# Attention pooling with divided GpSimd additions, pairwise additions instead of reductions on VectorE, and expert weights loaded from a later step

## The chip, the cores and the metric

The kernel runs on one core of a Trainium2 chip. The metric is device time in microseconds (us) of that core, from several executions; one further execution was profiled. The engines are TensorE (PE in the profile, its weight loads PEld), VectorE (DVE), ScalarE (ACT), GpSimd (POOL) and SyncE (SP), which here only issues DMA transfers. SBUF is the on-chip memory, PSUM the memory into which TensorE writes.

## The reference, cut to what matters

Attention over pooled keys and values is followed by a mixture of experts in which every token goes to one expert.

```python
# q, k, v: 8 batches, 8 heads, 576 tokens, 64 dims
k_p = k.reshape(B, H, 72, 8, D).mean(axis=3)      # 8 neighbours pooled
v_p = v.reshape(B, H, 72, 8, D).mean(axis=3)
attn = softmax(q @ k_p.T / sqrt(D))               # 576 x 72 for each head
x = (attn @ v_p) -> tokens x 512                  # 4608 tokens
logits = x @ w_gate; e_idx = argmax(logits, axis=1)
for e in range(8):
    out[e_idx == e] = gate * eom * (relu(x[e_idx == e] @ w1[e]) @ w2[e])
```

## The kernel before

The program has two parts. The first, written in one long order by hand (`attention_and_routing`, up to about 194 us of the profile), computes attention for 36 tiles of 128 tokens and finds each token's expert. The second (`experts`) runs the expert matmuls, for about 460 us.

The first part walks half-steps: tile i, half a of the heads (a is 0 or 1). In one half-step TensorE makes the scores of a tile, transposes the probabilities of the tile two steps back, and multiplies those of three steps back with the pooled values. VectorE takes the row maximum `m` (L242), the reciprocal `grec` (L280) and the normalised output `xg` (L286); ScalarE takes the exponentials. What is not part of every half-step is put between: `plan` holds functions by step (`at(step, f, ...)`), and `queue` holds generators of VectorE work (`pooled`, `route`) from which `work(n)` takes the next n pieces at three places of a half-step. A batch has 4.5 steps; batch b begins at step f.

Pooling of a batch b from 1 on is done as follows.

- Keys lie as 128 partitions x 4 head pairs x 8 positions x 72 columns (`k_t[b]`, named kq in the trace). `pool_k` on GpSimd (L181, L182, step f - 5.5) adds the upper half of the positions to the lower, three times, in place.
- Values lie as 128 partitions x 2 halves of the heads x 3 chunks x 512 columns (`vt`, named rows in the trace; 512 is 8 positions x 64 dims). `halve_v` on GpSimd (L196, step f - 2.5) adds positions 4 to 7 to 0 to 3, one addition for each half of the heads. `pooled` then reduces the four remaining positions on VectorE, one `tensor_reduce` for each chunk and half (`pool_v`, L199), six pieces of `queue` from step f - 2.
- `vt` is one buffer for all batches, so the loads of the next batch's values (`load_v`, L166) wait on SyncE for the last of these reductions, and the loads of q and k behind them in SyncE's order wait too.

Batch 0 is pooled by VectorE alone (`ready_k`, `first_v`), since nothing else can run before. The routing of a group of four tiles (`route`) is a chain of small VectorE operations: among them `d` (L307) and `cand` (L311), both with two inputs in SBUF, and the scalar addition to `gden` (L336). When it has found the places, GpSimd scatters the group's rows to memory (L395, an indirect DMA each).

`stage_in` (L410) loads 512 KB pieces of the first expert's weights into six stage buffers; their split into two parts by ScalarE and VectorE begins at step 26.

Of the kernel before, what the change touches and what calls it, by code (L numbers as in the profile page):

```python
# [15 lines left out]
ALU = mybir.AluOpType  # L16
AX = mybir.AxisListType
PSUM = bass.MemoryType.PSUM

B, H, S, D = 8, 8, 576, 64  # L20
# [57 lines left out]
def attention_and_routing(ctx, tc, sh, qT, kT, v, wg, wst, xs):  # L78
    nc = tc.nc
# [12 lines left out]
    vt = sh.rows[:, 0:6 * DM].rearrange("p (a c f) -> p a c f", a=2, c=3)  # L92
# [61 lines left out]
    k_t, vp_t, vT_t = {}, {}, {}  # L154
# [20 lines left out]
        nc.sync.dma_start(k_t[0][:, 2:4], k[:, 2:4])  # L175
        nc.sync.dma_start(q_t[0][:, :, P:S], q[:, :, P:S])

    def pool_k(b, eng, c0=0, c1=4):
        k = k_t[b][:, c0:c1]
        for w in (4, 2):  # L180
            eng.tensor_tensor(k[:, :, 0:w], k[:, :, 0:w], k[:, :, w:2 * w], op=ALU.add)  # L181
        eng.tensor_tensor(k[:, :, 0], k[:, :, 0], k[:, :, 1], op=ALU.add)  # L182

    def scale_k(b, c0=0, c1=4):
        for h in range(2):
# [3 lines left out]
    def ready_k(a):  # L189
        pool_k(0, nc.vector, 2 * a, 2 * a + 2)  # L190
        scale_k(0, 2 * a, 2 * a + 2)

    def halve_v(b):
        vp_t[b] = p2.tile([P, 3, 2, D], F32, tag="vp", name=f"vp{b}", bufs=1)
        for a in range(2):
            nc.gpsimd.tensor_tensor(vt[:, a, :, 0:256], vt[:, a, :, 0:256], vt[:, a, :, 256:512], op=ALU.add)  # L196

    def pool_v(b, a, c, n=1, w=4):
        nc.vector.tensor_reduce(vp_t[b][:, c:c + n, a], vt[:, a, c:c + n, 0:w * D].rearrange("p c (r d) -> p c d r", r=w),  # L199
                                axis=AX.X, op=ALU.add)  # L200

    def first_v(a):
        if a == 0:
            vp_t[0] = p2.tile([P, 3, 2, D], F32, tag="vp", name="vp0", bufs=1)
        pool_v(0, a, 0, 3, 8)

    def place_v(b, c):
        for h in range(2):
# [261 lines left out]
    def at(step, f, *args):  # L470
        plan.setdefault(step, []).append((f, args))

    def pooled(b):
        for a in range(2):
            for c in range(3):
                pool_v(b, a, c)
                yield 0

    tick = [0]
# [15 lines left out]
    for b in range(1, B):  # L495
        f = S * b // P + 0.5 * (b % 2)
        at(f - 8.5, load_k, b)
        at(max(f - 5, 0), load_v, b)
        at(f - 4.5, load_q, b)
        at(f - 5.5, pool_k, b, nc.gpsimd)  # L500
        at(max(f - 2.5, 1.5), scale_k, b)
        at(f - 2.5, halve_v, b)
        at(f - 2, lambda b: queue.insert(0, [pooled(b), 0, -1]), b)
        for c in range(3):
            at(f - 0.5 + 0.5 * c, place_v, b, c)
        at(f - 0.5, turn_v, b)
        at(f + 1.5, gate_v, b)
    for c in range(STAGES):
        at(3 + 0.5 * c, stage_in, c)
    for c in range(8):  # L510
        at(26 + 1.5 * c, split_hi, c)
        at(27 + 1.5 * c, split_lo, c)
# [13 lines left out]
    prepare_counts()  # L526
    ready_k(0)
    first_v(0)
    at(-0.5, ready_k, 1)
    at(-0.5, first_v, 1)  # L530
    at(1.5, prepare_routing)
    for c in range(3):
# [603 lines left out]
def program():  # L1136
# [12 lines left out]
    with ExitStack() as st:  # L1149
# [27 lines left out]
        with tile.TileContext(nc) as tc:  # L1177
            with ExitStack() as ctx, tc.manual_schedule():
                attention_and_routing(ctx, tc, sh, qT, kT, v, wg, wst, xs)
# [24 lines left out]
```

## Time and profile before

| | |
|---|---|
| Time, 3 runs | median 656.69 us, 655.51 to 657.07 |
| Profiled execution | 657.38 us; its span, first to last instruction, 655.7 us |
| Mean granted TensorE clock | 0.987 |
| Busy over the whole span | PE 93%, PEld 84%, DVE 54%, ACT 40%, POOL 34% |

The span is what the views of the profile show; about 1.7 us lie around it. A share of busy time is a mean over two quite different parts: VectorE is busy 54% of the whole, but nearly without a gap in the first part, where the change lies.

### The profile page before, as it was taken

How to read it: one execution, taken by the hardware profiler on the slowest of the kernel's cores; microseconds unless marked ns; L12 is line 12 of the kernel's file. 1: busy time of each engine (PE TensorE's matmuls, PEld its weight loads, DVE VectorE, ACT ScalarE, POOL GpSimd, SP SyncE). 2: the span in 40 equal slices, each digit the busy share in tenths (PEclk: the TensorE clock that was granted, in tenths of full speed). 3: DMA queues.
4: the chain of work that ended last, by engine and by line, in shares of the span. 5: the costliest groups of instructions: out<-in, count | busy, mean ns of one | idle time of the engine just before them, and what ended most of it. 6: DMA issues, size and time to landing. Idle time of an engine off the chain costs nothing.

```text
span 655.7 us, 11906 instructions
## 1 busy us (share of the span) xinstructions
PE 606.7 (93%) x3715; PEld 553.3 (84%) x3716; DVE 357.3 (54%) x805; ACT 260.0 (40%) x693; POOL 220.6 (34%) x270
## 2 busy tenths in 40 slices
PE   0798898989978999999989999999999899999996
PEld 0697897888877999799788989989898798989895
DVE  5789999899883822578545513265133632222221
ACT  1776886888441511347244402244031421211110
POOL 3557558662532421231404222141213213030213
PEclk9999999999998999999989999999999899999999
DMA  9898687783545931467836422064204112020203
GB/s 258 278 305 289 205 292 276 254 251 114 169 159 191 321 109 44 149 214 254 286 127 233 133 92 73 32 212 141 96 1 158 33 44 93 16 76 32 77 32 90
DMA packets 28746, 101.72 MB, mean 155 GB/s; under 512 B 4735, under 2 KB 5759, under 8 KB 26882
## 3 DMA queue, kind: packets, MB, share of 16 engines
q1 hardware_dynamic: 18194, 61.93, 29.4%
q0 software_dynamic: 10480, 39.03, 17.5%
q14 instruction: 51, 0.42, 0.2%
q8 instruction: 21, 0.34, 0.2%
HBM read 79.67 MB, written 22.58 MB: 156 GB/s over the span
## 4 chain that ended last, share of the span: by engine, by line
PE 64%; issue 2%; DVE 1%; DMA 1%; ACT 0%; DVEq 0%; POOL 0%; ACTq 0%; POOLq 0%
PE p_y L854 31%; PE p_h L873 31%; PE p_x L835 2%; DMA stage<-wst 1%; DVE w1a L998 1%; PE p_y L835 0%; DVE w1b L998 0%; DVE rows L1004 0%; ACT w2b L945 0%; POOL out L1115 0%; ACT w1b L945 0%; ACT xt L938 0%; DVE ht L1011 0%; DVEq L803 0%; PE p_y L915 0%
## 5 line engine op out<-in xcount | busy, mean ns | idle before, releaser
L953 ACT ACTIVATE ht<-p_h 128x384 fp32r<-128x384 f32 (+1 forms) x104 | 46.9, 451 | 264.2 <-PE p_h L873 263.7
L873 PE MATMUL p_h<-xt,w1b 128*128 128x384 f32 (+1 forms) x736 | 117.0, 320 | 5.3 <-issue 5.3
L873 PEld LDWEIGHTS p_h<-xt,w1b 128*128 128x128 f32 x736 | 115.9, 192 | 6.6 <-issue 6.2
L1011 DVE SCALAR_TENSOR_TENSOR ht<-p_h,ht 128x384 fp32r<-128x384 f32 (+1 forms) x104 | 52.5, 505 | 112.9 <-ACT ht L953 112.8
L854 PE MATMUL p_y<-w2a,ht 128*128 128x512 f32 x456 | 108.2, 397 | 5.9 <-issue 4.0
L854 PE MATMUL p_y<-w2b,ht 128*128 128x512 f32 x480 | 111.1, 391 | 0.0
L854 PEld LDWEIGHTS p_y<-w2a,ht 128*128 128x128 f32 x456 | 86.6, 192 | 24.4 <-issue 6.5
L854 PEld LDWEIGHTS p_y<-w2b,ht 128*128 128x128 f32 x480 | 89.5, 188 | 18.4
L873 PE MATMUL p_h<-xt,w1a 128*128 128x256 f32 (+1 forms) x640 | 95.4, 310 | 2.5 <-DVE sums L1024 2.4
L873 PEld LDWEIGHTS p_h<-xt,w1a 128*128 128x128 f32 x640 | 94.3, 193 | 3.5 <-DVE sums L1024 2.6
L1004 DVE TENSOR_SCALAR rows<-p_y,sc 128x512 f32<-128x512 f32 x41 | 30.5, 750 | 120.5 <-PE p_y L854 120.1
L1115 POOL DMA_INDIRECT out<-rows,dst x41 | 41.6, 1015 | 126.1 <-DVE rows L1004 121.4
L247 ACT ACTIVATE p<-p_h,m 128x72 f32<-128x72 f32 x288 | 71.2, 364 | 25.6 <-DVE m L242 25.5
L264 PE MATMUL av<-vbd,pT 128*128 128x162 f32 (+1 forms) x480 | 74.5, 308 | 7.3 <-DVE xg L286 2.4
L264 PEld LDWEIGHTS av<-vbd,pT 128*128 128x128 f32 (+1 forms) x480 | 61.6, 181 | 11.2 <-issue 5.8
L1090 POOL DMA_INDIRECT rows<-xs,src x51 | 59.7, 1171 | 24.2 <-POOL src L1086 13.9
L286 DVE TENSOR_TENSOR xg<-av,grec 128x320 f32<-128x320 f32 x72 | 53.5, 743 | 1.2
L1085 POOL COPY nx<-rows 128x6 f32<-128x6 f32 x17 | 4.2, 245 | 144.7 <-PE p_y L835 71.2
L395 POOL DMA_INDIRECT xs<-xg,where x36 | 36.4, 1012 | 44.0 <-DVE where L350 19.3
L236 PE MATMUL p_h<-kbd,q_even 128*128 128x144 f32 (+1 forms) x160 | 29.3, 310 | 16.1 <-DMA q_even<-qT 12.6
L257 ACT ACTIVATE pT<-ptr 128x384 f32<-128x384 f32 x72 | 38.1, 529 | 4.2 <-PE ptr L256 4.0
L236 PEld LDWEIGHTS p_h<-kbd,q_even 128*128 128x128 f32 (+1 forms) x160 | 23.4, 195 | 17.5 <-issue 12.9
(171 smaller groups left out, 696.4 us busy)
## 6 DMA issues: line engine op xcount, KB each, us to landing
stage<-wst SPq DMA_DIRECT2D x64, 512.0 KB, 5.4
kq<-kT SPq DMA_DIRECT2D x7, 1152.0 KB
rows<-v SPq DMA_DIRECT2D x16, 288.0 KB
kq<-qT SPq DMA_DIRECT2D x4, 1152.0 KB
q_even<-qT SPq DMA_DIRECT2D x3, 1152.0 KB
rows<-v SPq DMA_DIRECT2D x8, 256.0 KB
rows<-v SPq DMA_DIRECT2D x8, 160.0 KB
kq<-kT SPq DMA_DIRECT2D x2, 576.0 KB
```

What stands on the lines that cost most here:

```text
L236: nc.tensor.matmul(s[r0:r0 + n, 144 * c:144 * c + 144], q_t[b][:, 2 * a + c, s0:s0 + n], kbd[b % 2][:, 2 * a + c, :], start=True, stop=True)
L247: nc.scalar.activation(pt[i % 3][:, 4 * a + h, 0:KEYS], sv[:, h], AF.Exp, bias=m[:, h:h + 1])
L257: nc.scalar.activation(pT_t[i][:, 3 * a:3 * a + 3, :], tr[:, 0:384].rearrange("p (c n) -> p c n", c=3), AF.Copy)
L264: nc.tensor.matmul(av[r0:r0 + n, COLS * c:COLS * c + 2 * COLS], pT[:, 3 * a + c, r0:r0 + n], vbd[b % 2][:, a, c].rearrange("p h f -> p (h ...
L286: nc.vector.tensor_tensor(xg[g][:, j, HALF * a:HALF * a + HALF].rearrange("p (f h) -> p h f", h=4), avv[:, :, 0:D + 16], grec[g][:, j, hs] ...
L395: ins = nc.gpsimd.indirect_dma_start(out=xs, out_offset=bass.IndirectOffsetOnAxis(ap=where, axis=0), in_=x.bitcast(I32), in_offset=None)
L854: i = mm(p_y[k], ht[:, h, f, P * k:P * k + P], w[:, part, o:o + DM], start=(f == 0 and part == 0 and h == 0), stop=(f == 7 and h == 1))
L873: i = mm(to, w[:, part, o:o + P], x, start=(d == 0 and k == 0), stop=(d == 3 and k == len(terms) - 1))
L953: act(ht[:, 0, f, 0:size * P], p_h[f % 3][:, 0:size * P], AF.Relu).then_inc(q["hh"], 1)
L1011: nc.vector.scalar_tensor_tensor(ht[:, 1, f, 0:n], src, 0.0, ht[:, 0, f, 0:n].bitcast(F32), op0=ALU.max, op1=ALU.subtract).then_inc(q["hl" ...
L1090: nc.gpsimd.indirect_dma_start(out=xb[:, k].bitcast(I32), out_offset=None, in_=xs, in_offset=bass.IndirectOffsetOnAxis(ap=src[:, k:k + 1], ...
L1115: nc.gpsimd.indirect_dma_start(out=out, out_offset=bass.IndirectOffsetOnAxis(ap=dst[:, k:k + 1], axis=0), in_=yb[k], in_offset=None, bound ...
```

## The change

Three things change, and with them the order in which `queue` hands its pieces to VectorE.

1. `pool_k` on GpSimd makes its first two rounds as one addition for each head pair (`apart=1`): four additions of 288 columns and four of 144 where there was one of 1152 and one of 576. The third round stays one addition. `halve_v` makes six additions of 256 columns where there were two of 768.
2. `pool_v` on VectorE no longer reduces over a strided view. It adds the upper half of the columns to the lower: for batches 1 to 7 two additions for each half of the heads (3 x 128 columns, then 3 x 64 columns into `vp`), four pieces of `queue` instead of six; for batch 0 (`first_v`) three additions of 3 x 256, 3 x 128 and 3 x 64 columns instead of one reduction of 1536 columns.
3. The six `stage_in` are called at steps 14, 15.5, ... 21.5 instead of 3, 3.5, ... 5.5.

```diff
-    def pool_k(b, eng, c0=0, c1=4):
-        k = k_t[b][:, c0:c1]
-        for w in (4, 2):
-            eng.tensor_tensor(k[:, :, 0:w], k[:, :, 0:w], k[:, :, w:2 * w], op=ALU.add)
-        eng.tensor_tensor(k[:, :, 0], k[:, :, 0], k[:, :, 1], op=ALU.add)
+    def pool_k(b, eng, c0=0, c1=4, apart=0):
+        for w in (4, 2, 1):
+            n = apart if apart and w > 1 else c1 - c0
+            for c in range(c0, c1, n):
+                k = k_t[b][:, c:c + n]
+                eng.tensor_tensor(k[:, :, 0:w], k[:, :, 0:w], k[:, :, w:2 * w], op=ALU.add)
...
         for a in range(2):
-            nc.gpsimd.tensor_tensor(vt[:, a, :, 0:256], vt[:, a, :, 0:256], vt[:, a, :, 256:512], op=ALU.add)
-
-    def pool_v(b, a, c, n=1, w=4):
-        nc.vector.tensor_reduce(vp_t[b][:, c:c + n, a], vt[:, a, c:c + n, 0:w * D].rearrange("p c (r d) -> p c d r", r=w),
-                                axis=AX.X, op=ALU.add)
+            for c in range(3):
+                nc.gpsimd.tensor_tensor(vt[:, a, c, 0:256], vt[:, a, c, 0:256], vt[:, a, c, 256:512], op=ALU.add)
+
+    def pool_v(b, a, n):
+        to = vt[:, a, :, 0:n] if n > D else vp_t[b][:, :, a]
+        nc.vector.tensor_tensor(to, vt[:, a, :, 0:n], vt[:, a, :, n:2 * n], op=ALU.add)
...
-        pool_v(0, a, 0, 3, 8)
+        for n in (4 * D, 2 * D, D):
+            pool_v(0, a, n)
...
         for a in range(2):
-            for c in range(3):
-                pool_v(b, a, c)
+            for n in (2 * D, D):
+                pool_v(b, a, n)
                 yield 0
...
-        at(f - 5.5, pool_k, b, nc.gpsimd)
+        at(f - 5.5, pool_k, b, nc.gpsimd, 0, 4, 1)
...
     for c in range(STAGES):
-        at(3 + 0.5 * c, stage_in, c)
+        at(14 + 1.5 * c, stage_in, c)
```

On VectorE, around the pooling of batch 7, the order before was this (`m` is the row maximum, `grec` and `xg` normalise the output, `vp` takes the pooled values, `w1a` is a part of the expert's weights, `lg` and `mx` begin a group's routing):

```order
L242 TENSOR_REDUCE m_1_1940<-p_h 128x4
L199 TENSOR_REDUCE vp_1907<-rows 128x64 x2
L280 RECIPROCAL grec_1729<-av_1_1944 128x4
L199 TENSOR_REDUCE vp_1907<-rows 128x64
L286 TENSOR_TENSOR xg_1727<-av_1_1944,grec_1729 128x4x80
L199 TENSOR_REDUCE vp_1907<-rows 128x64
L425 TENSOR_TENSOR w1a<-stage,w1a 128x512
L242 TENSOR_REDUCE m_0_1969<-p_h 128x4
L199 TENSOR_REDUCE vp_1907<-rows 128x64 x2
L280 RECIPROCAL grec_1979<-av_0_1973 128x4
L301 TENSOR_REDUCE lg_1981<-xg_1727 128x64
```

With the change the same place reads:

```order
L245 TENSOR_REDUCE m_1_2002<-p_h 128x4
L202 TENSOR_TENSOR rows<-rows 128x3x128
L202 TENSOR_TENSOR vp_1965<-rows 128x3x64
L283 RECIPROCAL grec_1787<-av_1_2006 128x4
L202 TENSOR_TENSOR rows<-rows 128x3x128
L289 TENSOR_TENSOR xg_1785<-av_1_2006,grec_1787 128x4x80
L202 TENSOR_TENSOR vp_1965<-rows 128x3x64
L428 TENSOR_TENSOR w1a<-stage,w1a 128x512
L245 TENSOR_REDUCE m_0_2031<-p_h 128x4
L304 TENSOR_REDUCE lg_2033<-xg_1785 128x64
L308 TENSOR_REDUCE mx_2035<-lg_2033 128x4
```

The pooling ends one half-step earlier, and each of its instructions now has two inputs in SBUF; the routing behind it moves up.

On GpSimd, around the halving of batch 4's values, with what each instruction waits for (names in capitals are semaphores of DMA queues; Pool is GpSimd's own), the order before was:

```order
L395 DMA xs<-xg_489,where_866 38913x642
L196 TENSOR_TENSOR rows<-rows 128x3x256 [waits DMAHW5_49,DMAHW6_49,DMAHW4_49,DMAHW7_49,DMAHW1_49,DMAHW0_49]
L196 TENSOR_TENSOR rows<-rows 128x3x256
L395 DMA xs<-xg_734,where_1083 38913x642 [waits DVE_49]
L181 TENSOR_TENSOR kq<-kq 128x4x288 [waits DMAHW3_49,Activation_49]
L181 TENSOR_TENSOR kq<-kq 128x4x144 [waits Pool_49]
L182 TENSOR_TENSOR kq<-kq 128x4x72 [waits Pool_49]
```

With the change it is:

```order
L398 DMA xs<-xg_501,where_878 38913x642
L198 TENSOR_TENSOR rows<-rows 128x256 [waits DMAHW7_49,DMAHW6_49]
L198 TENSOR_TENSOR rows<-rows 128x256 [waits DMAHW1_49,DMAHW0_49]
L198 TENSOR_TENSOR rows<-rows 128x256 [waits DMAHW3_49,DMAHW2_49]
L198 TENSOR_TENSOR rows<-rows 128x256 x3
L398 DMA xs<-xg_754,where_1117 38913x642 [waits DVE_49]
L183 TENSOR_TENSOR kq<-kq 128x288 [waits DMAHW5_49,Activation_49]
L183 TENSOR_TENSOR kq<-kq 128x288 x3
L183 TENSOR_TENSOR kq<-kq 128x144 [waits Pool_49] x4
L183 TENSOR_TENSOR kq<-kq 128x4x72 [waits Pool_49]
```

Nothing changes its place on GpSimd here. The additions of one round now follow each other without depending on each other.

On SyncE's queue, behind the load of batch 2's keys, the order before was (stage is a piece of expert weights, rows a piece of v, q_even q, kq keys):

```order
L158 DMA kq<-kT 128x2304
L147 DMA xs<-stage 1x642
L410 DMA stage<-wst 128x1024 x2
L166 DMA rows<-v 72x2x512
L166 DMA rows<-v 32x2x512
...
L166 DMA rows<-v 72x2x512
L410 DMA stage<-wst 128x1024
L162 DMA q_even<-qT 128x2304
L410 DMA stage<-wst 128x1024
L158 DMA kq<-kT 128x2304
L410 DMA stage<-wst 128x1024 x2
```

With the change these stage loads are gone from here; three stand behind the keys of batch 5, as below, and three behind those of batch 6.

```order
L162 DMA q_even<-qT 128x2304
L158 DMA kq<-kT 128x2304
L413 DMA stage<-wst 128x1024 x3
L166 DMA rows<-v 72x2x512
```

Two loads of 512 KB no longer stand ahead of the values of batch 2, and four no longer around its q and the keys of batch 3.

## Rows read from the trace of the kernel before

**Rows 1.** Busy time by stretch, windows view; (x) counts instructions.
```profile
40.00:60.00 20.00, 17.77 (x143) 15.67 (x143) 18.94 (x54) 13.78 (x52) 10.40 (x7) 1.00 0.89 289
60.00:160.00 100.00, 92.75 (x754) 85.01 (x752) 95.82 (x302) 80.11 (x303) 61.12 (x52) 1.00 0.73 243
```

**Rows 2.** Groups by line and form, VectorE, 19 to 166 us: busy, mean ns | idle.
```profile
L199 DVE TENSOR_REDUCE vp<-rows 128x64 f32<-128x256 f32 x42 | 23.6, 591 | 2.0 <-POOL rows L196 1.9
...
L307 DVE TENSOR_TENSOR d<-lg,mx 128x32 f32<-128x32 f32 x8 | 8.6, 1077 | 0.0
...
L336 DVE TENSOR_SCALAR gden<-gden 128x4 f32<-128x4 f32 x7 | 5.0, 713 | 0.0
...
L311 DVE SCALAR_TENSOR_TENSOR cand<-d,rev 128x32 f32<-128x32 f32 x7 | 3.4, 487 | 0.0
...
L319 DVE TENSOR_TENSOR zs<-lg,oh 128x32 f32<-128x32 f32 x7 | 1.3, 190 | 0.0
```

**Rows 3.** The same view of GpSimd, 19 to 166 us.
```profile
L196 POOL TENSOR_TENSOR rows<-rows 128x768 f32<-128x768 f32 x14 | 25.1, 1818 | 10.4 <-DMA rows<-v 6.6 <-DVE m L242 2.9 <-issue 0.8
L181 POOL TENSOR_TENSOR kq<-kq 128x1152 f32<-128x1152 f32 x7 | 18.5, 2641 | 20.2 <-DMA kq<-kT 20.1
L181 POOL TENSOR_TENSOR kq<-kq 128x576 f32<-128x576 f32 x7 | 9.9, 1414 | 0.5
L182 POOL TENSOR_TENSOR kq<-kq 128x288 f32<-128x288 f32 x7 | 5.6, 797 | 0.5
```

**Rows 4.** The same view of VectorE, 0 to 19 us.
```profile
L199 DVE TENSOR_REDUCE vp<-rows 128x192 f32<-128x1536 f32 x2 | 5.5, 2750 | 5.3 <-DMA rows<-v 5.3
...
L181 DVE TENSOR_TENSOR kq<-kq 128x576 f32<-128x576 f32 x2 | 1.5, 745 | 0.0
L181 DVE TENSOR_TENSOR kq<-kq 128x288 f32<-128x288 f32 x2 | 0.9, 457 | 0.1
```

**Rows 5.** Timeline from 69.7 us: start, duration, engine; like rows merged (xN).
```profile
69.74 2.65 POOL L181 TENSOR_TENSOR kq<-kq 128x1152 f32<-128x1152 f32 x1 [3.35 <-DMA kq<-kT]
...
70.40 1.13 DVE L199 TENSOR_REDUCE vp<-rows 128x64 f32<-128x256 f32 x2
```

**Rows 6.** Timeline from 44.4 us.
```profile
44.46 1.81 POOL L196 TENSOR_TENSOR rows<-rows 128x768 f32<-128x768 f32 x1 [6.65 <-DMA rows<-v]
...
44.93 1.39 DVE L307 TENSOR_TENSOR d<-lg,mx 128x32 f32<-128x32 f32 x1
```

**Rows 7.** Timeline from 62.8 us.
```profile
62.82 3.57 POOL L196 TENSOR_TENSOR rows<-rows 128x768 f32<-128x768 f32 x2
...
63.08 3.37 DVE L307 TENSOR_TENSOR d<-lg,mx 128x32 f32<-128x32 f32 x1
...
67.31 0.41 PE L264 MATMUL av<-vbd,pT 128*128 128x162 f32 x1 [1.57 <-DVE vbd L224]
```

**Rows 8.** Timeline from 101.9 us.
```profile
102.02 3.80 DVE L336 TENSOR_SCALAR gden<-gden 128x4 f32<-128x4 f32 x1
...
102.21 3.58 POOL L196 TENSOR_TENSOR rows<-rows 128x768 f32<-128x768 f32 x2
...
106.83 0.38 PE L264 MATMUL av<-vbd,pT 128*128 128x162 f32 x1 [2.10 <-DVE at L345]
```

**Rows 9.** Timeline from 143.3 us.
```profile
143.42 3.61 POOL L196 TENSOR_TENSOR rows<-rows 128x768 f32<-128x768 f32 x2
...
145.29 1.14 DVE L199 TENSOR_REDUCE vp<-rows 128x64 f32<-128x256 f32 x2
```

**Rows 10.** Timeline from 22.2 us.
```profile
19.59 4.13 POOL L181 TENSOR_TENSOR kq<-kq 128x1152 f32<-128x1152 f32 x2 [10.86 <-DMA kq<-kT]
...
22.76 1.04 DVE L148 CAST tri<-stage 128x128 bf16<-128x128 f32 x1
```

**Rows 11.** Waits of GpSimd, 27 to 75 us: total, times, longest.
```profile
POOL kq L181 <- DMA kq<-kT: 9.3, 3, 4.4
POOL rows L196 <- DMA rows<-v: 6.6, 1, 6.6
```

## The prediction

> **What bounds the kernel now.** I looked first at where the change lies in time: all of it is in the first part, up to about 166 us. The windows view of that part [rows 1] says what bounds it. From 40 to 160 us TensorE is busy 17.77 + 92.75 = 110.5 of 120 us and VectorE 18.94 + 95.82 = 114.8. Both are nearly full, so TensorE can win at most its 9.5 us of idle time there: 2.2 between 40 and 60 us, 7.25 later. The waits view puts nearly all of these on VectorE, in small pieces but for two: 1.57 us at 67.31 [rows 7] and 2.10 us at 106.83 [rows 8].
>
> Next I asked why VectorE is full. In the view by line and form [rows 2] the 42 reductions of pooled values take 23.6 us. Beside them stand small operations with absurd means: `d`, 32 columns, takes 1077 ns on average, while `zs`, the same shape with two SBUF inputs, takes 190. The excess over 190 ns is 8 x 0.89 = 7.1 us for `d`, 7 x 0.30 = 2.1 for `cand`, 7 x 0.52 = 3.7 for `gden`: 12.9 us in all that isn't work.
>
> The timelines say what it is. At 44.93 `d` takes 1.39 us and ends at 46.32, just behind the end (46.27) of a GpSimd addition [rows 6]. At 63.08 `d` takes 3.37 and ends at 66.45, behind the second of two GpSimd additions (66.39) [rows 7]; at 102.02 `gden` takes 3.80 and ends at 105.82, again behind the second (105.79) [rows 8]. The cast at 22.76 is the same picture [rows 10]. So such an operation of VectorE is held while GpSimd adds. A strided reduction is not: at 70.40 two of them take 1.13 us in the middle of a GpSimd addition that runs from 69.74 to 72.39 [rows 5].
>
> This cuts into the change from both sides. It takes 42 instructions that are never held and puts 28 in their place that have two SBUF inputs, like `d`. And it divides the GpSimd instructions that hold.
>
> **The change part by part.**
>
> *VectorE's own work.* An addition with two SBUF inputs took 457 ns for 288 columns and 745 for 576 [rows 4]: 1.00 ns a column and 0.169 us fixed. That gives 0.94 us for 768 columns, 0.55 for 384, 0.36 for 192. A batch's six reductions cost 6 x 0.591 = 3.55 us [rows 2]; four additions cost 2 x (0.55 + 0.36) = 1.83. That is 1.72 less for each of seven batches, 12.0 us of VectorE. For batch 0, 2.75 us [rows 4] become 0.94 + 0.55 + 0.36 = 1.85 without gaps; dependent additions add some 0.04 each, so 0.83 less, twice: 1.65 us.
>
> *The start, -1.1 us.* Both of those reductions stand on VectorE ahead of a row maximum for which ScalarE waits, while GpSimd is still idle (its first addition starts at 19.59 [rows 10]), so nothing holds them. But the cast at 22.76 [rows 10] comes next, and it was released when the second GpSimd addition ended. The first GpSimd addition starts when its keys land, no earlier than now; four additions of 288 columns at 0.80 [rows 3] end at 22.8. The cast would get through at 22.8 instead of 23.8. Bounds: -1.65 (not held) to 0 (held to the end of the second round too, 24.7); I take -1.1.
>
> *The values and keys of batches 2 and 3, -1.5 us.* GpSimd waited 6.6 us for values once and 9.3 in three waits for keys between 27 and 75 us [rows 11], behind the stage loads. These waits cost nothing directly, since pooling is scheduled well ahead. But with 1 MB less in front, the additions on batch 3's keys move ahead of the pooling of batch 2, which they now cover in part, and that pooling is 1.72 us shorter. Of the 2.23 us that TensorE idles between 40 and 60 I give back 1.5. Bounds: -2.2 to 0 (the keys come earlier and hold `d` instead).
>
> *Pooling elsewhere, -0.4 us.* In batches 4 and 5 little or no GpSimd addition lies at the pooling, and the 1.72 us less counts where TensorE waits: in the small pieces, 7.25 - 1.57 - 2.10 = 3.6 us. I take 0.4; bounds 0 and -1.5.
>
> *The new additions held, 0.* In batch 7 the pooling began at 145.29, when the first half's addition was done and the second half's ran until 147.03 [rows 9]; the reductions ran through. The new additions would be held by three pieces of 0.73 us (below): 0.7 to 2.2 us, and I take 1.5. Less the 1.72 saved, that is nothing. Batches 1 and 6 are alike. In batch 3 the pooling lies inside the additions on keys [rows 5]: four pieces of 0.80, held up to 3.2 us, 1.6 in the middle, again nothing net. Bounds for the five places together: -6 (not held) to +5.
>
> *The divided additions on GpSimd.* From 797 ns for 288 columns and 1414 for 576 [rows 3], 2.14 ns a column and 0.18 us fixed: 0.49 us for 144 columns, 0.73 for 256. A batch's keys go from 4.85 to 4 x 0.80 + 4 x 0.49 + 0.80 = 5.96 us, its values from 3.64 to 6 x 0.73 = 4.38: 1.85 us more, 13 us in all. GpSimd is busy 61 of 100 us [rows 1], so this alone costs nothing. What it does to the holds depends on one thing: whether VectorE gets in between two GpSimd additions that follow without a gap. Three times it stood there waiting. Once it got in [rows 6], twice not [rows 7, 8]. Taking one in three, an operation that arrives at the beginning of `halve_v` waits 0.5 + 2 x 0.73 = 2.0 us, where 63.08 and 102.02 waited 3.2 and 3.6. TensorE's two waits of 1.57 and 2.10 would shrink by 1.2 and 1.6. Since the halving also moves against the routing (1.85 us longer a batch, scatters between), I count half of it: -1.4. Bounds: -3.7 and +1.4 (held to the end of all six, 0.7 longer each). For keys the first round grows from 2.64 to 3.2: +0.3.
>
> [...]
>
> *Stage loads at steps 14 to 21.5, 0.* They stand behind keys on SyncE's queue, ahead of values that wait there for VectorE anyway. At 0.73 DMA share from 60 to 160 us [rows 1] there is room for 3 MB, and their first reader is at step 26. If they made values late, GpSimd's slack (its 39 idle us of 100) covers it.
>
> *Sum.* -1.1 - 1.5 - 0.4 + 0 - 1.4 + 0.3 = -4.1. The profiled execution took 657.38 us, span 655.7 and 1.7 around it: 653.3. It lies 0.7 above the median of the runs shown, 656.69; against that the forecast is 652.6 us.
>
> **The rivals.**
>
> *First: VectorE gets in after every piece.* A wait is then at most 0.80 us. Waits grow with the square of the piece: 2.64, 1.41, 0.80 and 3.64 (squares 22.8) become four of 0.80, four of 0.49, 0.80 and six of 0.73 (7.4), so 12.9 us of holds fall to 4.2; new ones, 0.4 at five places, add 2. VectorE has 12.9 - 4.2 - 2 + 12.0 = 18.7 us less, TensorE's 9.5 us of waits mostly go (I take 6.6), and the start gives 1.6: 648.5. For it: rows 6; against it: rows 7, 8. [...]
>
> *Second, slower: VectorE never gets in before a gap.* Keys then hold for 3.2 + 1.96 = 5.2 us (the second round's waits are on additions long done), values for 4.4. Squares: 26.6 + 0.6 + 19.2 = 46.4, twice 22.8, so 12.9 us become 26: +13.3. The pooling is held 2.2 us in batches 1 and 7, 1.6 in 6, 1 in 5, 2.6 in 3: 9.6. Less 12.0, VectorE has 10.9 us more. At 63.08 and 102.02 holds of 6.8 us made TensorE wait 3.67, a share of 0.54: +5.9, less 1.1 at the start: 661.5. It decides from about 2 us more VectorE time on. For it: rows 7, 8; against it: rows 6. [...]
>
> *Third: nothing reaches TensorE.* What VectorE saves is eaten by other holds, and only the start gains, in part: 656.0. Speaking for it is that TensorE itself is 92% busy.
>
> **How the numbers follow.** A change of 0.3% (2 us) is about what a measurement of this kernel can tell from none. The likeliest case 0.45, with 650 to 657 as its own range (three quarters of it below 654.7, a quarter between); the first rival 0.20, the second 0.21, the third 0.14. Faster: 0.34 + 0.20 + 0.02 = 0.56; same: 0.11 + 0.10 + 0.03 = 0.24; slower: 0.20. Leaving out a tenth at either end, the range is 648.3 to 661: to the first rival's time below, just short of the second's above.
>
> **What would show it.** At the start the second row maximum some 1.6 us earlier, and the cast released near 22.8. Four `L202` additions a batch at 0.55 and 0.36 us where GpSimd is idle; longer by whole pieces of 0.73 or 0.80 in batches 1, 3, 6, 7. The mean of `d` and `gden` falls below 1077 and 713 (first rival: under 450; second: over 1500). GpSimd's additions at 0.80, 0.49 and 0.73. TensorE idle from 40 to 160 us near 6.5 instead of 9.5. The prediction fails if VectorE's additions are held for 3 us and more in most batches, or if TensorE's idle time stays though the holds shrink.

## The result and the profile after

The changed kernel took 652.43 us in the median of 20 runs (646.45 to 656.90), the kernel before 656.47 us in as many beside it: a ratio of 0.9937, 95% interval 0.9916 to 0.9958. The forecast was 652.6 us, faster; on a second chip the ratio was 0.9911 (0.9877 to 0.9945). The time came out as forecast. Several terms of the sum did not, and the experiments below are about those.

The profiled execution took 649.39 us, span 647.5, so it is one of the quicker ones. The windows view answers to [rows 1] (columns: window, length, then busy time and instructions of PE, PEld, DVE, ACT and POOL, granted clock, DMA share, GB/s):

```profile
40.00:60.00 20.00, 19.33 (x162) 18.13 (x162) 19.25 (x63) 15.70 (x63) 16.09 (x23) 1.00 0.66 225
60.00:160.00 100.00, 92.14 (x756) 85.96 (x755) 87.76 (x287) 80.34 (x303) 68.71 (x92) 0.98 0.80 270
...
80.00:100.00 20.00, 18.44 (x148) 17.47 (x147) 18.62 (x63) 15.66 (x61) 15.60 (x22) 1.00 1.02 339
100.00:120.00 20.00, 17.81 (x153) 16.39 (x151) 14.57 (x48) 15.43 (x57) 13.77 (x21) 1.00 0.97 332
120.00:140.00 20.00, 18.70 (x140) 17.92 (x142) 18.77 (x59) 15.65 (x59) 16.54 (x22) 0.91 0.79 247
```

From 40 to 60 us TensorE gained 1.6 us of busy time. From 60 to 160 VectorE has 8 us less to do, but TensorE is no busier than before; the DMA engines are full from 80 to 120 us (share 1.02 and 0.97), and the clock, 1.00 in both stretches before, is 0.91 for 20 us.

VectorE at the start, the view by line and form from 0 to 19 us, beside [rows 4]:

```profile
L202 DVE TENSOR_TENSOR rows<-rows 128x768 f32<-128x768 f32 x2 | 1.9, 954 | 4.8 <-DMA rows<-v 4.8
...
L202 DVE TENSOR_TENSOR rows<-rows 128x384 f32<-128x384 f32 x2 | 1.1, 558 | 0.1
...
L202 DVE TENSOR_TENSOR vp<-rows 128x192 f32<-128x192 f32 x2 | 0.7, 357 | 0.1
```

The same view from 19 to 166 us, beside [rows 2]:

```profile
L202 DVE TENSOR_TENSOR rows<-rows 128x384 f32<-128x384 f32 x14 | 10.5, 752 | 5.4 <-POOL rows L198 5.4
L202 DVE TENSOR_TENSOR vp<-rows 128x192 f32<-128x192 f32 x14 | 7.1, 508 | 0.2
...
L310 DVE TENSOR_TENSOR d<-lg,mx 128x32 f32<-128x32 f32 x8 | 3.3, 411 | 0.0
...
L322 DVE TENSOR_TENSOR zs<-lg,oh 128x32 f32<-128x32 f32 x8 | 2.6, 322 | 0.0
...
L339 DVE TENSOR_SCALAR gden<-gden 128x4 f32<-128x4 f32 x8 | 1.8, 222 | 0.0
L314 DVE SCALAR_TENSOR_TENSOR cand<-d,rev 128x32 f32<-128x32 f32 x8 | 1.7, 208 | 0.0
...
L148 DVE CAST tri<-stage 128x128 bf16<-128x128 f32 x1 | 0.4, 391 | 0.0
```

The pooling takes 10.5 + 7.1 = 17.6 us where the reductions took 23.6. Unheld, as at the start, it would be 14 x (0.558 + 0.357) = 12.8, so 4.8 us are holds. The operations that stood out before have shrunk (`d` 1077 to 411 ns, `gden` 713 to 222); `zs` has grown from 190 to 322. That is one execution: in another of the same kernel (e9 below) `d` took 1287.

GpSimd in the same stretch, beside [rows 3]:

```profile
L198 POOL TENSOR_TENSOR rows<-rows 128x256 f32<-128x256 f32 x42 | 30.9, 769 | 3.4 <-DMA rows<-v 3.3
...
L183 POOL TENSOR_TENSOR kq<-kq 128x288 f32<-128x288 f32 x35 | 27.9, 821 | 20.5 <-DMA kq<-kT 13.3 <-ACT p L250 6.6
L183 POOL TENSOR_TENSOR kq<-kq 128x144 f32<-128x144 f32 x28 | 13.4, 506 | 0.0
```

Its waits from 27 to 75 us, beside [rows 11] (line, what it waited for: total, times, longest): the 9.3 and 6.6 us behind DMA are now 2.6 and 0.2.

```profile
POOL kq L183 <- ACT p L250: 6.6, 2, 3.9
POOL kq L183 <- DMA kq<-kT: 2.6, 1, 2.6
...
POOL rows L198 <- DMA rows<-v: 0.2, 1, 0.2
```

The row maximum `m`, once a half-step, dates the lead over before. In these two executions it was 2.9 us at step 6, 8.5 at step 11.5 (the hold of [rows 7] is gone) and 11.8 at step 21 (that of [rows 8] is gone). At step 26 it was 10.6, half a step later 6.8, and 5.5 at the end of the tiles. The other 2.6 us between the two spans lie behind the last row maximum; from there to the end the 14 profiled executions of this document vary from 487.3 to 490.4 us. What took the lead back from step 26 on is on TensorE's timeline (start, duration, engine; idle time before, with its releaser, in brackets):

```profile
116.81 0.99 PE L267 MATMUL av<-vbd,pT 128*128 128x162 f32 x6
120.96 1.10 PE L239 MATMUL p_h<-kbd,q_even 128*128 128x144 f32 x4 [3.16 <-DMA q_even<-qT]
```

And the windows of 2 us there:

```profile
118.00:120.00 2.00, 0.00 (x0) 0.00 (x0) 1.68 (x2) 0.00 (x0) 2.00 (x4) 1.00 1.00 420
120.00:122.00 2.00, 1.04 (x5) 1.06 (x6) 1.48 (x5) 0.00 (x0) 1.84 (x2) 0.79 0.42 175
122.00:124.00 2.00, 2.00 (x10) 2.00 (x9) 1.97 (x6) 1.47 (x6) 1.39 (x3) 0.50 0.63 176
124.00:126.00 2.00, 2.00 (x16) 1.96 (x15) 1.97 (x8) 1.41 (x8) 1.97 (x3) 0.85 0.93 281
126.00:128.00 2.00, 2.00 (x18) 2.00 (x17) 1.90 (x9) 2.00 (x9) 2.00 (x4) 1.00 1.02 301
```

TensorE waits 3.16 us for q (an earlier wait for q, 1.49 us at 98.80, had no lower clock behind it), then works at a granted clock of 0.50 until 124.6 us. In busy time that second loss is invisible: a full 2 us hold 10 matmuls from 122 us on, at 0.50, and 18 from 126, at 1.00.

### The profile page after: what moved, and what is told of

It is laid out like the page before. It is cut to its first block, busy times and chain, and to the rows that moved or that the text cites. A ratio compares the mean times of both kernels' runs of the same rounds, so it can differ in the third digit from the quotient of the medians.

```text
span 647.5 us, 11966 instructions
## 1 busy us (share of the span) xinstructions
PE 603.8 (93%) x3715; PEld 553.9 (86%) x3716; DVE 344.5 (53%) x795; ACT 259.6 (40%) x693; POOL 233.5 (36%) x340
## 4 chain that ended last, share of the span: by engine, by line
PE 67%; issue 2%; DVE 1%; DVEq 0%; POOL 0%; ACT 0%; POOLq 0%
PE p_y L857 33%; PE p_h L876 32%; PE p_x L838 2%; DVE w1a L1001 1%; PE p_y L838 0%; POOL out L1118 0%; DVE rows L1007 0%; DVE xt L994 0%; ACT xt L941 0%; PE p_y L918 0%; DVE sums L1027 0%; DVEq L689 0%; DVEq L1026 0%; DVEq L1038 0%; DVEq L806 0%
## 5 line engine op out<-in xcount | busy, mean ns | idle before, releaser
L876 PE MATMUL p_h<-xt,w1b 128*128 128x384 f32 (+1 forms) x736 | 115.5, 317 | 4.8 <-issue 4.8
L876 PEld LDWEIGHTS p_h<-xt,w1b 128*128 128x128 f32 x736 | 114.4, 189 | 6.1 <-issue 5.7
L1093 POOL DMA_INDIRECT rows<-xs,src x51 | 57.8, 1134 | 24.6 <-POOL src L1089 13.2
L183 POOL TENSOR_TENSOR kq<-kq 128x288 f32<-128x288 f32 (+1 forms) x63 | 41.0, 681 | 20.5 <-DMA kq<-kT 13.3
L239 PEld LDWEIGHTS p_h<-kbd,q_even 128*128 128x128 f32 (+1 forms) x160 | 24.2, 202 | 19.7 <-issue 15.9
```

Source lines behind the costliest of these rows:

```text
L239: nc.tensor.matmul(s[r0:r0 + n, 144 * c:144 * c + 144], q_t[b][:, 2 * a + c, s0:s0 + n], kbd[b % 2][:, 2 * a + c, :], start=True, stop=True)
L876: i = mm(to, w[:, part, o:o + P], x, start=(d == 0 and k == 0), stop=(d == 3 and k == len(terms) - 1))
L1093: nc.gpsimd.indirect_dma_start(out=xb[:, k].bitcast(I32), out_offset=None, in_=xs, in_offset=bass.IndirectOffsetOnAxis(ap=src[:, k:k + 1], ...
```

## The experiments

Each kernel was run on one chip with the kernel before beside it; the ratio is to that. Before took 656.5 us in the median on the first chip and 662.2 to 662.7 on the three others (e1 to e4, e5 to e8 and e9 to e12 on one each), so only ratios are compared. Where two ratios are subtracted, the interval of the difference comes from the two half-widths, added as squares. "Pooling" is the busy time of VectorE's pooling, "d" the mean of `d`, both from 19 to 166 us of the one profiled execution.

| Kernel | GpSimd divided | VectorE adds pairs | Stage loads | Ratio (95%) | Pooling, us | d, ns |
|---|---|---|---|---|---|---|
| before | no | no | 3 to 5.5 | 1 | 23.6 | 1077 |
| e2 | no | no | late | 0.9960 (0.9931 to 0.9989) | 23.5 | 694 |
| e3 | yes | no | 3 to 5.5 | 0.9946 (0.9922 to 0.9969) | 23.2 | 940 |
| e4 | no | yes | 3 to 5.5 | 1.0015 (0.9989 to 1.0041) | 24.9 | 868 |
| e7 | no | yes | late | 1.0020 (0.9995 to 1.0045) | 23.9 | 721 |
| e12 | values only | yes | late | 0.9935 (0.9909 to 0.9961) | 23.2 | 577 |
| changed | yes | yes | late | 0.9937 (0.9916 to 0.9958) | 17.6 | 411 |
| e9, changed again | yes | yes | late | 0.9911 (0.9877 to 0.9945) | 16.9 | 1287 |
| e1 | yes | yes | 3 to 5.5 | 0.9897 (0.9861 to 0.9934) | 15.9 | 671 |
| e5 | yes | yes | spread | 0.9904 (0.9875 to 0.9934) | 16.7 | 745 |
| e6 | yes | yes | last | 0.9880 (0.9842 to 0.9917) | 16.0 | 573 |
| e8 | keys chained | yes | late | 0.9854 (0.9817 to 0.9890) | 17.0 | 397 |
| e10 | keys chained | yes | last | 0.9863 (0.9831 to 0.9894) | 16.8 | 370 |
| e11 | keys chained | yes | spread | 0.9858 (0.9819 to 0.9897) | 17.6 | 323 |

**The parts one by one.** The theory: dividing GpSimd's additions is what gains, and late loads cost; the rivals are that one of the others gains.

e1_early_loads, on the changed kernel:

```diff
-        at(14 + 1.5 * c, stage_in, c)
+        at(3 + 0.5 * c, stage_in, c)
```

> The changed kernel with part 3 undone: the six stage loads are at steps 3 to 5.5 again. Theory (part 3 costs): moved to steps 14 to 21.5 the loads fill the DMA engines (share 1.02 from 80 to 100 us and 0.97 from 100 to 120), q of a late batch lands late, TensorE waits 3.2 us for it and then loses its clock (0.91 from 120 to 140 us). Put back, these go: share from 80 to 120 us near 0.8, no wait on qT over 1 us, 647 to 650 us, 2 to 5 below the changed kernel's 652.4. Rival (part 3 helps): without the late loads the keys and values of batches 2 and 3 are late again, as in rows 11, and the 2.4 us that the changed kernel gained around step 5 go: 654 to 656 us. As predicted (stage loads cost nothing, gain 1.5 us early): 654.

The ratio lies in the theory's range (647 to 650 of 656.5), but not for its reason. A wait for q is there again, at another place (TensorE's timeline, then windows):

```profile
64.30 0.31 PE L239 MATMUL p_h<-kbd,kq 128*64 128x144 f32 x1 [2.68 <-DMA kq<-qT]
```

```profile
62.00:64.00 2.00, 0.00 (x0) 0.00 (x0) 1.74 (x3) 1.61 (x7) 2.00 (x4) 1.00 1.02 417
64.00:66.00 2.00, 1.70 (x15) 1.45 (x16) 1.44 (x5) 0.08 (x1) 1.47 (x2) 0.71 0.89 358
66.00:68.00 2.00, 2.00 (x9) 1.66 (x10) 1.74 (x10) 1.12 (x5) 0.00 (x0) 0.50 0.58 205
```

Here too the DMA engines are full ahead of the wait (share 1.02 from 62 to 64 us) and the clock is halved behind it (0.50 from 66 to 68). So with the loads at either of these two places a late q was possible once the first part ran ahead.

e2_late_loads_alone, on before:

```diff
-        at(3 + 0.5 * c, stage_in, c)
+        at(14 + 1.5 * c, stage_in, c)
```

> The kernel before with part 3 alone (stage loads at steps 14 to 21.5). Theory: the early stretch wins some 1.5 to 2.5 us, the stretch from 100 to 140 us loses 3 to 5 by a late q: 657 to 660 us, a little slower than 656.5. Rival (part 3 is where the gain is): 653 or less. The holds stay as in before: mean of d near 1077 ns, gden near 713.

A miss: faster, not slower. From 40 to 60 us TensorE is busy 19.82 us instead of the 17.77 of [rows 1]; no wait of TensorE for q reached 1 us. The holds did not stay either: `d` fell to 694 ns and `gden` to 548, though nothing was divided. So these means move without a division too; each is of seven or eight operations of one execution.

e3_divided_alone, on before, with the changed `pool_k`:

```diff
-            nc.gpsimd.tensor_tensor(vt[:, a, :, 0:256], vt[:, a, :, 0:256], vt[:, a, :, 256:512], op=ALU.add)
+            for c in range(3):
+                nc.gpsimd.tensor_tensor(vt[:, a, c, 0:256], vt[:, a, c, 0:256], vt[:, a, c, 256:512], op=ALU.add)
...
-        at(f - 5.5, pool_k, b, nc.gpsimd)
+        at(f - 5.5, pool_k, b, nc.gpsimd, 0, 4, 1)
```

> The kernel before with part 1 alone: GpSimd's additions divided, VectorE still reduces. Theory (VectorE gets in between two GpSimd additions): the means of d and gden fall below 450 and 350 ns, cand below 300, TensorE's waits of 1.57 and 2.10 us on VectorE go, 650 to 653 us. Rival (VectorE gets in only at a gap or a wait, and the changed kernel escaped because its routing fell elsewhere): d and gden stay at 1000 and 700 ns or more, and the time at 656 to 659.

The time is 0.54% less, at the weak end of the theory's range. `gden` fell to 360 ns and `cand` to 184, but `d` stayed at 940: the theory is right for most operations and wrong for `d`, which at 131.09 us was held 3.56 us, past five boundaries between additions of keys. TensorE then waited 3.4 us, and the waits behind VectorE that were to go left one of 1.5 us behind `vbd`, at 83.03.

e4_pairs_alone, on before, with the changed `pool_v`:

```diff
-        pool_v(0, a, 0, 3, 8)
+        for n in (4 * D, 2 * D, D):
+            pool_v(0, a, n)
...
-            for c in range(3):
-                pool_v(b, a, c)
+            for n in (2 * D, D):
+                pool_v(b, a, n)
```

> The kernel before with part 2 alone: pairwise additions on VectorE beside whole GpSimd additions. Theory (holds last as long as a GpSimd instruction, or two): the additions by VectorE save 12 us when nothing holds them (0.55 and 0.36 us each), but in batches 1, 3, 6 and 7 they are held for 1 to 3 us at a time, so that their mean lies over 0.9 us and about half of the 12 us is lost: 653 to 656 us. Rival (part 2 is the whole gain): means near 0.55 and 0.36, and 648 to 651 us. Rival the other way (never in before a gap): 658 or more.

No gain at all. The view by line and form shows why, and the timeline one case of it:

```profile
L200 DVE TENSOR_TENSOR rows<-rows 128x384 f32<-128x384 f32 x14 | 12.9, 919 | 0.8 <-POOL rows L196 0.7
L200 DVE TENSOR_TENSOR vp<-rows 128x192 f32<-128x192 f32 x14 | 12.0, 858 | 0.2
```

```profile
69.69 4.32 POOL L181 TENSOR_TENSOR kq<-kq 128x1152 f32<-128x1152 f32 x2 [4.22 <-ACT pT L258]
...
70.08 2.67 DVE L200 TENSOR_TENSOR vp<-rows 128x192 f32<-128x192 f32 x1
...
72.77 1.66 DVE L200 TENSOR_TENSOR rows<-rows 128x384 f32<-128x384 f32 x1
...
75.20 1.06 PE L265 MATMUL av<-vbd,pT 128*128 128x162 f32 x6 [2.64 <-DVE xg L287]
```

Additions of 0.36 and 0.55 us take 2.67 and 1.66 inside GpSimd's additions on keys, where two reductions ran through in 1.13 [rows 5]. In all, 24.9 us instead of 23.6: the whole saving went into holds. What TensorE lost is more than these 1.3 us. The windows view from 40 to 160 us, beside [rows 1]:

```profile
40.00:60.00 20.00, 17.73 (x133) 16.10 (x132) 17.96 (x49) 14.71 (x58) 11.07 (x8) 0.91 0.86 294
...
60.00:160.00 100.00, 89.58 (x700) 83.39 (x699) 88.84 (x268) 73.41 (x276) 60.10 (x50) 0.95 0.72 239
```

TensorE idled 12.7 us instead of 9.5, and its granted clock was 0.91 and 0.95 where before had 1.00 (0.85 and 0.94 in e7 below). This was one of e4's slower executions, 666.1 us beside a median of 663.0.

e7_pairs_late_undivided, on the changed kernel, with `pool_k` as before:

```diff
-        at(f - 5.5, pool_k, b, nc.gpsimd, 0, 4, 1)
+        at(f - 5.5, pool_k, b, nc.gpsimd)
...
-            for c in range(3):
-                nc.gpsimd.tensor_tensor(vt[:, a, c, 0:256], vt[:, a, c, 0:256], vt[:, a, c, 256:512], op=ALU.add)
+            nc.gpsimd.tensor_tensor(vt[:, a, :, 0:256], vt[:, a, :, 0:256], vt[:, a, :, 256:512], op=ALU.add)
```

> The changed kernel with part 1 undone: GpSimd's additions whole again, pairwise additions on VectorE and late loads kept. Theory (part 1 is what makes part 2 pay, by short holds): VectorE's pairwise additions take 0.8 to 0.9 us on average as with part 2 alone, d 800 ns or more, and the time is 0.996 to 1.002 of before. Rival (parts 2 and 3 alone give the gain): 0.994 or less.

As the theory had it: 1.002, pooling means 1106 and 600 ns (`d` lower than expected). Parts 2 and 3 without part 1 gain nothing.

**Which division.** e12_values_divided_only, on the changed kernel:

```diff
-        at(f - 5.5, pool_k, b, nc.gpsimd, 0, 4, 1)
+        at(f - 5.5, pool_k, b, nc.gpsimd)
```

> The changed kernel with whole additions on keys again (1152 and 576 columns) and divided ones on values. Theory (holds cost by the length of a piece, wherever it is): VectorE's pairwise additions in batches 3 and 4 stand inside additions of keys of 2.6 us, as with part 2 alone; mean of the 384-column addition 0.85 us or more, d 700 ns or more, and about half of the gap between the changed kernel (0.994) and the undivided one (1.002) is lost: 0.996 to 1.000. Rival (the division of values carries the gain): 0.995 or less. Rival (that of keys does): 1.000 or more.

The rival wins: with divided values alone the time is that of the changed kernel. The pooling does stand in the keys' long additions, as expected (`d`, 577 ns, came out lower),

```profile
L202 DVE TENSOR_TENSOR rows<-rows 128x384 f32<-128x384 f32 x14 | 15.7, 1123 | 0.9 <-POOL rows L198 0.9
L202 DVE TENSOR_TENSOR vp<-rows 128x192 f32<-128x192 f32 x14 | 7.5, 536 | 0.2
```

yet dividing the keys as well gained no time that these runs can tell. e9 shows what can eat it.

**The same kernel again.** e9_changed_again is the changed kernel without an edit.

> The changed kernel itself, unaltered, beside the next three on one chip. Two questions. First, its time against these: 0.991 to 0.997 of before. Second, its first part: the profiled execution of the changed kernel was 11 us ahead of before at 113 us and lost some 5 of them behind a wait of 3.2 us for q. Theory (q can't come earlier than the DMA engines bring it, so this repeats): again a wait for q of over 1 us between 60 and 125 us with half clock behind it. Rival (that execution was an uncommonly quick one, and the wait came of its lead): a lead of 5 to 8 us at 113 us and no wait for q over 1 us.

The ratio, 0.9911, lies at the lower end of the expected range, and of the two accounts of the wait the rival holds: the lead at step 22.5 (113 us before) was 6.1 us against the same trace of before, which is from another chip, and there was no wait for q over 1 us. It had another loss instead (timeline):

```profile
127.41 4.68 DVE L310 TENSOR_TENSOR d<-lg,mx 128x32 f32<-128x32 f32 x1
127.68 5.70 POOL L183 TENSOR_TENSOR kq<-kq 128x288 f32<-128x288 f32 x9
...
132.87 0.88 PE L267 MATMUL av<-vbd,pT 128*128 128x162 f32 x2 [3.98 <-DVE cand L314]
```

```profile
130.00:132.00 2.00, 0.00 (x0) 0.00 (x0) 2.00 (x1) 0.00 (x0) 2.00 (x4) 0.77 1.05 350
132.00:134.00 2.00, 1.13 (x4) 1.16 (x5) 1.97 (x10) 1.88 (x8) 1.40 (x4) 0.50 1.07 302
134.00:136.00 2.00, 2.00 (x10) 1.99 (x9) 1.97 (x7) 2.00 (x10) 0.00 (x0) 0.50 0.93 334
136.00:138.00 2.00, 2.00 (x14) 1.94 (x13) 0.76 (x5) 2.00 (x9) 0.00 (x0) 0.52 0.27 111
```

`d` waits through six boundaries of the divided additions, longer than any single hold of before, and gets in at the seventh. Divided additions that follow without a gap can act like one long one: `d` took 4.68 us here.

**A gap between the additions.** e8_chained_keys, on the changed kernel: the additions on keys go head pair by head pair, so that most need the one before. The edit also divides the third round, into four additions of 72 columns.

```diff
-        for w in (4, 2, 1):
-            n = apart if apart and w > 1 else c1 - c0
-            for c in range(c0, c1, n):
+        n = apart if apart else c1 - c0
+        for c in range(c0, c1, n):
+            for w in (4, 2, 1):
```

> The changed kernel with GpSimd's divided additions of keys in another order: head pair by head pair (288, 144, 72 columns, each needing the one before) instead of round by round. In the traces so far VectorE always got in where GpSimd waited some 0.08 us between two additions, and of the ungapped boundaries inside the keys it missed about a third. Theory (a gap decides): no operation of VectorE is held past a boundary that has a gap of 0.08 us, so that none of 32 columns takes more than 1.7 us and d comes below 400 ns; 0.989 to 0.994 of before, since one hold less of 1 us is little beside the noise. Rival (it is chance, or what stands behind on GpSimd decides): d is still held past two and more boundaries in a batch.

Every hold inside the keys ends at its first boundary (one less than 0.05 us behind an operation's start is not counted here and below). In the timeline three operations of one routing stand in one series of keys and get through in about half a microsecond each; the longest of all operations of 32 columns up to 166 us takes 1.13 us:

```profile
92.68 4.37 POOL L183 TENSOR_TENSOR kq<-kq 128x144 f32<-128x144 f32 x8
...
93.78 0.60 DVE L310 TENSOR_TENSOR d<-lg,mx 128x32 f32<-128x32 f32 x1
...
95.54 0.57 DVE L318 TENSOR_TENSOR oh<-cand,best 128x32 bf16<-128x32 f32 x1
...
96.15 0.53 DVE L322 TENSOR_TENSOR zs<-lg,oh 128x32 f32<-128x32 f32 x1
```

The gain is more than expected: 0.9854. It is the lowest ratio measured; its interval lies below the changed kernel's first one and overlaps that of e9, from which it differs by 0.0057 (0.0007 to 0.0107). Where the gain comes from is argued, not shown. This profile is no better than the changed kernel's first (TensorE idle 9.4 us from 40 to 160, against 8.5; `d` 397 ns, against 411), only better than e9's (12.7 us and 1287 ns), so the long holds that no longer occur are the likely cause. No run divides the third round without the chain.

**Where the loads go.** e5_loads_spread, on the changed kernel:

```diff
-        at(14 + 1.5 * c, stage_in, c)
+        at(5.5 + 4.5 * c, stage_in, c)
```

> The changed kernel with its six stage loads one by one, each behind a batch's keys (steps 5.5, 10, ... 28), instead of three and three behind the keys of batches 5 and 6. Theory (stage loads next to each other make q late: in the changed kernel TensorE waits 3.2 us for q at 117.8 us and then runs at half clock, with the loads early it waits 2.7 us at 61.6 and then the same): no wait of TensorE for q above 0.5 us between 40 and 160 us, no half clock behind one, and a time of 0.985 to 0.990 of before (the changed kernel 0.994). Rival (a faster first part meets another wait in place of this one, as long): 0.992 to 0.996.

e6_loads_last, on the changed kernel:

```diff
-        at(14 + 1.5 * c, stage_in, c)
+        at((19, 23.5, 27.5, 28, 28.5, 29)[c], stage_in, c)
```

> The changed kernel with its stage loads as late as their readers allow: steps 19 and 23.5, and four behind the last q (27.5 to 29), where the changed kernel's DMA share was 0.33. Theory: as with the loads spread, 0.985 to 0.990 of before, DMA share below 0.9 in every stretch of 20 us from 40 to 140 us. Rival (the loads are now too late for their split, which begins at step 26): a wait of ScalarE or VectorE on stage between 130 and 180 us, and 0.992 or more.

From 40 to 160 us neither waits for q (e5 waits 1.05 us for it at 28.65). Their ratios, 0.9904 (just above the range expected) and 0.9880 (in it), are below the changed kernel's, but the intervals overlap, and e1, which does wait for q, lies at 0.9897. Whether the place of the loads matters is not settled on this base. The rival of e6 did not come: no wait on the stage buffers shows from 130 to 180 us. e6's DMA share reached 0.93 from 100 to 120 us, more than expected, and e5's as well.

e10_chained_loads_last joins the `stage_in` line of e6 to the `pool_k` of e8, e11_chained_loads_spread that of e5.

> Keys added head pair by head pair (as e8) and stage loads as late as their readers allow (as e6), in one kernel. If the two gains add up (0.985 and 0.988 where the changed kernel is at 0.994): 0.979 to 0.984 of before. If both remove the same thing, or are noise of a few profiles: 0.985 to 0.990. No operation of 32 columns is held past a boundary with a gap.

> Keys added head pair by head pair and the stage loads one behind each batch's keys (as e5). As for the kernel with the loads last: 0.980 to 0.986 if the gains add up, 0.986 to 0.990 if not; and within 0.4% of the loads-last kernel either way, since both take the loads out of the way of q.

0.9863 and 0.9858 beside 0.9854 with the loads left late: with chained keys the place of the loads makes no difference that these runs can tell. e10 lies where the gains do not add up, e11 at the border of its two ranges. All three chained kernels lie together.

## Why the forecast was right, and which of its terms were not

The sum, -4.1 us, was met: (1 - 0.9937) x 656.5 = 4.1. Its terms were not those that made it.

**Price of the additions: right.** 954, 558 and 357 ns against 0.94, 0.55 and 0.36; GpSimd's pieces 821, 506 and 769 ns against 0.80, 0.49 and 0.73, the excess being time in which VectorE held them (undisturbed they took 0.79 to 0.82, 0.48 to 0.50 and 0.72 to 0.74, those of 288 and 256 columns 1.04 to 1.11 where a 384-column addition had got in).

**The start, -1.1: near.** The second row maximum came 1.66 us earlier, 1.6 were announced, and the cast began at 22.35 and took 0.39, near the 22.8. Single executions spread: in the eleven with the new start it came 0.82 to 2.18 us earlier than in before, 1.5 in the mean, and in e2 and e3, where the start is untouched, 0.72 and 0.07. Half a step later the eleven were 1.0 us ahead in the mean, and e2 and e3 as before.

**Pairwise additions: about as forecast, but only beside divided ones.** Start, batches 2 and 3 and other pooling were to gain 3.0 together, the new holds being paid for. Beside part 1 they did: from e3 (0.9946) to e1 (0.9897), on one chip, part 2 gains 0.49%, 3.2 us (0.4 to 6.1). Alone it gave +0.15%, or 1.0 us more (0.7 less to 2.7 more, x 662). The forecast let five batches be held for what they saved, 5 x 1.72 us, and the others not at all. With divided additions the 28 new instructions take 3.1 (e1) to 4.8 us more than unheld, less than that; with whole ones 24.9 - 12.8 = 12.1 us, which is all of the 12.0 that they save.

**Divided additions, -1.4 + 0.3: the step that failed, as too small.** Alone they gave -0.54%, 3.6 us (2.1 to 5.2), and beside part 2 more: from e4 (1.0015) to e1 (0.9897), on one chip, 1.18%, 7.8 us (4.8 to 10.8). The forecast took "VectorE gets in one time in three" from three cases. The count over the 14 profiled executions, up to 166 us, is below: operations of VectorE that lasted over 1.2 times their shortest of that execution plus 0.08 us, and the first place in them where one GpSimd addition followed another. Other limits shift the counts by a few.

| Boundary between two GpSimd additions | got in | missed |
|---|---|---|
| any, with a gap of about 0.08 us (the second needs the first) | 74 | 0 |
| whole additions on values, no gap | 6 | 5 |
| divided additions on values, no gap | 98 | 1 |
| divided additions on keys, no gap | 44 | 18 |

So the first rival's mechanism (in after every piece) holds for the divided additions on values (98 of 99), and the second's (not before a gap) for a part of those on keys (18 of 62 missed); after a miss at the keys 28 of the next 46 boundaries were missed too. A gap let VectorE in 74 times of 74. Why the keys miss and the values hardly ever do no run here shows.

**Stage loads, 0, and batches 2 and 3, -1.5: right alone, not on top of the rest.** Part 3 alone gave -0.40%, 2.6 us (0.7 to 4.6), with TensorE 2.05 us busier from 40 to 60 us; that is what the term of 1.5 described. "Room for 3 MB" was read from a mean DMA share of 0.73 over 100 us, while the six loads fall into 40 us, where the share then was 1.02 and 0.97. In the first profiled execution q was late there, in the other (e9) it wasn't, and on top of the other two parts moving the loads gained nothing (0.9937 and 0.9911, against e1's 0.9897 without it). That the loads made q late is likely, not shown: by the trace's packets (stage pieces come in 4096 bytes, q and keys in 9216) the second three pieces moved from 96 to 109 us, and q, issued at 109.10, behind them from 110 to 121; and in e5 and e6, with the loads elsewhere, no wait for q shows from 40 to 160.

**TensorE's idle time from 40 to 160 us was to fall from 9.5 to 6.5.** It was 120 - 111.47 = 8.5, and 12.7 in e9. So the forecast's own sign of failing, idle time that stays though the holds shrink, came for the greater part. Waits of 3 to 4 us, for q or for a held `d`, came in place of those of [rows 7, 8], and the halved clock behind them (0.50), not in the sum at all, took by estimate, as busy time times the share of the clock not granted, some 1.5 us (1.04 x 0.21 + 2 x 0.50 + 2 x 0.15, from the windows) and in e9 2.5 us (1.13 x 0.50 + 2 x 0.50 + 2 x 0.48).

So the forecast was right in part by luck: the divided additions gained some 2.5 us more than their terms (3.6 alone, against 1.1), and against that stood the late loads, whose 2.6 us alone did not come on top of the others, and a loss that was left out (the clock). The parts measured alone add up to -0.54 + 0.15 - 0.40 = -0.79%, near the whole, but that is chance too: parts 1 and 2 together give -1.03% (e1), where their sum alone is -0.39%. The holds tie the parts together.

## What to carry to other kernels

Pieces that GpSimd works off without a gap are not yet pieces for VectorE (inside the keys 18 of 62 such boundaries were missed, inside the divided values 1 of 99): order them so that each needs the one before, which here left a gap of about 0.08 us, and VectorE gets in between, 74 times of 74 here (the kernel so ordered, its third round divided too, has 0.9854 instead of 0.9937 and 0.9911). Additions with two SBUF inputs in place of a reduction are to be priced with their holds: here 24.9 us beside whole GpSimd additions and 15.9 to 17.6 beside divided ones, against 12.8 unheld and 23.6 for the reductions. Two changes that meet in the same waits are not to be added up from runs of each alone: part 2 gained nothing alone (1.0015) and 0.49% beside part 1. One profiled execution dates a wait well but doesn't say how often it occurs: the same kernel lost its lead to a late q in one and to a held `d` in the next.

## What the runs showed of the hardware that was not expected

A wait on TensorE can cost twice: the granted clock fell to 0.50 behind waits of 3.16 (changed) and 2.68 us (e1), and in a wait of 3.98 us (e9), after which TensorE worked on at 0.50 (0.52 in the mean from 136 to 138 us). The length of the wait alone doesn't tell: at one place of the program (`av` behind `vbd`) e10 waited 1.72 us at 79.45 and had 0.50 from 80 to 82 us, while e9 waited 2.30 at 80.91 and had 1.00 from 78 to 86; e12 waited 3.10 us at 50.86 and had 1.00 from 50 to 58.

While VectorE is let in, GpSimd is held in turn: in the changed kernel's profile its 256-column additions took 0.72 to 0.74 us undisturbed and 1.04 to 1.06 us where a 384-column addition of VectorE had got in ahead of them.
